# Attention beside a dense layer: a group's 64 scores in ten phases of six and seven instead of eleven phases

## The chip, the cores and the metric

The kernel runs on one core of a Trainium2 chip. The metric is the device time of one execution in microseconds (us). The program is one launch; it starts and ends with data in the chip's main memory.

## What is computed

The reference mixes two branches over the same input `x` of 2048 tokens by 512 channels: softmax attention with 32 heads of 16 channels (A), and a token-mixing MLP (B), with a gate per token.

```
qkv = x @ wqkv                                  # 32 heads, Dh = 16
scores = einsum("bhqd,bhkd->bhqk", q, k) * Dh**-0.5
o = einsum("bhqk,bhkd->bhqd", softmax(scores), v)
a = o_in_rows @ wo                              # (1, 2048, 512)

h = layernorm(x)
u = gelu(einsum("bsd,sf->bdf", h, w1) + b1)     # over tokens: 2048 -> 1792
b = einsum("bdf,fs->bds", u, w2) + b2           # 1792 -> 2048, transposed back

g = sigmoid((x * gate_w).sum(-1))
out = g * a + (1 - g) * b
```

All inputs and the output are fp32.

## The kernel before

Products that need fp32 accuracy are made of three matmuls of numbers split into a high and a low part (`hi`, `lo`). The kernel first makes v, then q and k in split form (written to main memory), then the first MLP layer with its GELU. All the rest, from about 300 us to 1290 us, is one stage in which the attention runs beside the second MLP layer and most of the output projection. The change lies in this stage alone.

*Groups.* There are `NG` = 32 groups: 16 pairs of heads times two halves of the queries. A group has 64 scores. A score (line 804) is one matmul of 64 rows: 128 keys by 512 queries of one head `i`. Head 0 sits on rows 0 to 63 of the array and head 1 on rows 64 to 127 (`i * HALF`), so a score uses half of the rows.

*Dense matmuls.* The second MLP layer and the output projection (tile `dn`, line 844) are issued as steps. Each step runs twice, once on either half of the rows, both adding to one PSUM bank. The list `dense` says which steps go with which *two*, a two being two consecutive phases; the first phase of a two (`second` = 0) runs the steps on rows 64 to 127 beside scores of head 0, the second phase the other way round. `put` fills the list, with a list of sizes per tile: `sizes_of` gives six or four for the second layer, `put_outputs` six for the projection's parts, and four at the end, where each of the last eight tiles sums the first `EARLY` = 8 of its 12 projection matmuls; `others` (line 887) does the remaining four after the attention. There are `TWOS` = 5 twos in a group, so ten phases, and behind them an eleventh phase of four scores without dense matmuls: 10 x 6 + 4 = 64.

*A phase on PE.* First its scores, each followed by a dense matmul on the other half of the rows. Where a phase has fewer dense matmuls than scores, the first scores run alone, on alternating halves. Then `apply_v` takes the exponentials of the phase before (`late`): a score's exponentials times v, two matmuls of 256 columns (line 768, 17 output rows each). Two units (scores) of the two query blocks make a pair, whose eight matmuls use four column strips of the array. The result gathers in one PSUM tile `av`, which is copied out once a group by DVE (line 731). When the phase of four has been issued, two of the three pairs that wait are taken, and the third moves on to the next phase.

*A phase on ACT.* Two scores fill one tile `s` of `ps_s`, that is two PSUM banks of 512 columns. One exponential (line 813, 128 x 1024) turns it into a tile `pt`. `ps_s` has three such tiles and `pt` six. `open_s` carries a half-filled tile from score to score.

The order of all instructions of the stage is written out by hand (`tc.manual_schedule`): each engine runs its queue in this order and waits by semaphores. POOL writes a one-element `token` after a phase's last dense matmul, and the next phase's first one waits for it, so that the two halves of the rows don't add to one bank at once.

Of the kernel before, what the change touches and what calls it, by code (L numbers as in the profile page):

```python
# [1 line left out]

# [7 lines left out]
F32 = mybir.dt.float32  # L10
# [3 lines left out]
AF = mybir.ActivationFunctionType  # L14
# [44 lines left out]
def gated_mix(ctx: ExitStack, tc: tile.TileContext, a_x, a_wqkv, a_wo, b_w1, b_b1, b_w2, b_b2, gate_w, out):  # L59
# [278 lines left out]
    with tc.tile_pool(name="ln0", bufs=3, side="right") as ln:  # L338

        def project(w, n):  # L340
            ps = bank()
            cols = slice(n * NB, (n + 1) * NB)
            hi, lo = w
            products(ps, [((hi[:, k, :], lo[:, k, :]), (xt_hi[:, k, cols], xt_lo[:, k, cols])) for k in range(ND)])
            return ps
# [178 lines left out]
    o_d = [[dram.tile([P, QW], F32, name=f"o{h}{k}") for k in range(ND)] for h in range(2)]  # L524
    r_d = [[dram.tile([P // DH, QW], F32, name=f"r{h}{k}") for k in range(ND)] for h in range(2)]
    ptp_ctx = ExitStack()
    ptp = ptp_ctx.enter_context(tc.tile_pool(name="pt", bufs=6, reuse_waits="tile"))
    psum_ctx = ExitStack()
    ps_s = psum_ctx.enter_context(tc.tile_pool(name="ps_s", bufs=3, space=PSUM, reuse_waits="tile"))
    ps_dn = psum_ctx.enter_context(tc.tile_pool(name="ps_dn", bufs=1, space=PSUM, reuse_waits="tile"))  # L530
    ps_av = psum_ctx.enter_context(tc.tile_pool(name="ps_av", bufs=1, space=PSUM, reuse_waits="tile"))
    o_parts = {}
# [97 lines left out]
    def project(t, n, m):  # L630

        box = []

        def load():
            if m == EARLY:
                row = end.tile([P, D], F32, name=f"base{t}")
            else:
                row = out_pool.tile([P, D], F32, name="row", bufs=3)
            rows[t] = load_row(row, part_d[t] if n else bp_d[t])

        def step(i):
            if i == 0:
                box.extend((ps_dn.tile([P, D], F32, name="dn"), list(o_matmuls(t // NH, t, n, m))))

            def done():
                output(t, box[0], rows[t])
                if m == 3 * ND:
                    nc.sync.dma_start(of[t * P : (t + 1) * P, :], rows[t])
                elif m != EARLY:
                    nc.sync.dma_start(part_d[t], rows[t])  # L650

            return box[0], *box[1][i], i == 0, i == m - n - 1, done if i == m - n - 1 else None

        return [(step, i) for i in range(m - n)], load

    TWOS = 5
    dense, calls = {}, {}  # L660

    def put(steps, at, sizes):
# [6 lines left out]
    def call(at, *what):  # L669
        calls.setdefault(at, []).append(what)  # L670

    def put_outputs(tiles, n, m, at, sizes=None):
        for t in tiles:
            steps, load = project(t, n, m)
            call(at - 1, load)
            at = put(steps, at, sizes or [m - n])
        return at

    def sizes_of(at, n, fours):

        sizes = [6] * n
        for i in [i for i in reversed(range(n)) if (at + i) % TWOS][:fours]:
            sizes[i] = 4
        return sizes

    EARLY = 8
    part_d = [dram.tile([P, D], F32, name=f"part{t}") for t in range(NS)]
    for k in range(ND):
        call(3 * k + 2, load_wo, k)
# [1 line left out]
    first, at = steps[:28], put(steps[28:], 0, [8, 6])  # L691
    for t in range(NS):
        if t:
            at = put(second_layer(t), at, sizes_of(at, 9, 6) if t > 9 else sizes_of(at, 8, 3))
        if t == 7:
            call(at - 8, fetch_o, 0, 0)
            call(at - 5, fetch_o, 0, 1)
            at = put_outputs(range(NH), 0, 6, at)
        if t == 10:
            call(at - 8, fetch_o, 0, 2)  # L700
            call(at - 5, fetch_o, 0, 3)
            at = put_outputs(range(NH), 6, 12, at)
    call(at - 8, fetch_o, 1, 0)
    call(at - 5, fetch_o, 1, 1)
    assert at - 5 > (NP + 8) * TWOS + 4
    call(at, open_end)
    at = put_outputs(range(NS - 3, NS), 0, 4, at)
    assert at == (NP + 12) * TWOS + 7
    call(at - 3, fetch_o, 1, 2)
    at = put_outputs(range(NH, NS - 3), 0, EARLY, at, [4, 4])  # L710
    at = put_outputs(range(NS - 3, NS), 4, EARLY, at)
    assert at == NG * TWOS
    call((NG - 1) * TWOS + 2, fetch_o, 1, 3, 3)

# [37 lines left out]

    added = [0, 0]

    def pairs_of(g, units, last):

        pairs = list(zip(*([u for u in units if u[2] == qb] for qb in range(2))))
        return [(g, pair, last and n == len(pairs) - 1) for n, pair in enumerate(pairs)]

    def apply_v(pairs):  # L760
        ot = None
# [19 lines left out]
    with tc.manual_schedule(engines=engines):  # L781
        kt, qt = {0: load_k(0)}, {0: load_q(0)}
        late, open_s, fence = [], None, None

        for n, (step, *args) in enumerate(first):
            if n and n % 12 == 0:
                split_weight(nc.vector.tensor_copy, nc.vector.tensor_tensor)
            ps, a, b, start, stop, done = step(*args)
            nc.tensor.matmul(ps, a, b, start=start, stop=stop)  # L789
            if done:  # L790
                done()

        def score(grp, i, n, done):

            nonlocal open_s
            c, qb = n // 2, (n + i) % 2
            if open_s is None:
                open_s = ps_s.tile([P, 2, NB], F32, name="s"), ptp.tile([P, 2, NB], F32, name="pt")
                m = 0
            else:  # L800
                m = 1
            s, pt = open_s
            rows = slice(i * HALF, i * HALF + ROWS)
            nc.tensor.matmul(  # L804
                s[:, m, :],
                kt[grp][rows, c * P : (c + 1) * P],
                qt[grp][rows, qb * NB : (qb + 1) * NB],
                start=True,
                stop=True,
            )  # L810
            done.append((i, c, qb, pt[:, m, :]))
            if m:
                nc.scalar.activation(pt, s, AF.Exp, scale=SCALE)  # L813
                open_s = None

        for grp in range(NG):
            at = [0, 0]
            for ph in range(2 * TWOS + 1):
                if ph == 0 and grp + 1 < NG:
                    qt[grp + 1] = load_q(grp + 1)  # L820
                if ph == 1 and grp + 1 < NG:
                    kt[grp + 1] = load_k(grp + 1)
                two, second = divmod(ph, 2)
                two += grp * TWOS
                if ph == 2 * TWOS:
                    n_s, beside = 4, []
                elif second:
                    n_s = 6
                else:
                    for what, *args in calls.get(two, ()):  # L830
                        what(*args)
                    n_s, beside = 6, [step(*args) for step, *args in dense.get(two, ())]
                units = []
                for n in range(n_s - len(beside)):
                    i = (n + second + 1) % 2
                    score(grp, i, at[i], units)
                    at[i] += 1
                half = slice(0, HALF) if second else slice(HALF, P)
                for m, (ps, a, b, first, last, done) in enumerate(beside):

                    if not 4 <= m < len(beside) - 2 or len(beside) <= n_s:
                        score(grp, second, at[second], units)
                        at[second] += 1
                    mm = nc.tensor.matmul(ps, a[half], b[half], start=first and not second, stop=last and bool(second))  # L844
                    if m == 0 and fence is not None:
                        tc.add_manual_dep(mm.ins, fence.ins.name, SYNC, reason=REASON)
                    if m == len(beside) - 1:
                        fence = nc.gpsimd.memset(token, 0.0)  # L848
                        tc.add_manual_dep(fence.ins, mm.ins.name, SYNC, reason=REASON)
                    if done and second:  # L850
                        done()
                if grp == ph == 0:
                    shift_rows(nc.vector, k_bufs[1])
                if second:
                    while stores:
                        stores.pop()()
                    if len(ready) < 2:
                        split_weight(nc.vector.tensor_copy)
                    for n, (ready_at, step) in enumerate(slow):
                        if ready_at <= two:  # L860
                            slow.pop(n)[1]()
                            break

                n = 2 if ph == 2 * TWOS and grp < NG - 1 else len(late)
                apply_v(late[:n])
                late = late[n:] + pairs_of(grp, units, ph == 2 * TWOS)
        last_ot = apply_v(late)
    psum_ctx.close()

# [3 lines left out]
    with (  # L873
# [8 lines left out]
        def others(*tiles, m=0, n=3 * ND):  # L882

            for t in tiles:
                mms = list(enumerate(o_matmuls(1, NH + t, EARLY, 3 * ND)))
                for i, (a, b) in mms[m:n]:
                    nc.tensor.matmul(pa[t], a, b, start=i == 0 and t not in LATE, stop=i == len(mms) - 1 and t in LATE)  # L887

# [142 lines left out]
```

## Time and profile before

| | |
|---|---|
| time, median of 3 runs | 1308.93 us (1307.51 to 1309.08) |
| time of the profiled execution | 1307.55 us |
| span of the profiled execution | 1305.8 us, granted TensorE clock 0.999 |
| PE (matmul) busy | 1299.0 us, 99% |
| ACT busy | 1090.6 us, 84% |
| DVE, POOL busy | 403.9 us, 200.0 us |
| exponentials | 1024 of 128 x 1024, 962.5 us busy |
| scores, av, dense halves | 2048, 8192 and some 1600 matmuls |

The span is the time from the first to the last instruction; the time of an execution has a little more around it. Busy times of PE are of a pipelined engine: a matmul's row begins at its start and ends when its last column is through, so that rows of neighbours overlap. The distance from start to start says more than the duration.

### The profile page before, as it was taken

The page shows a single profiled execution, that of the slowest core. Times are in us where ns is not written, and L with a number is a line of the kernel's source. Part 1 is how long each engine was busy: PE and PEld are TensorE (multiplying, and loading weights), DVE is VectorE, ACT ScalarE, POOL GpSimd, SP SyncE. Part 2 cuts the span into 40 slices and gives each one's busy share as a digit, 9 for nine tenths or more (in the row PEclk, how much of TensorE's full clock was granted, in tenths as well). Part 3 has the DMA queues.
Part 4 walks back from the last instruction along what each step waited for, and adds up shares of the span by engine and source line. Part 5 has one row for each costly group of instructions (what it writes and reads, how often), then busy time and mean ns, then how long its engine had stood idle before and what let it go on. Part 6 is the DMA issues. An engine that isn't in the chain of part 4 may idle for free.

```text
span 1305.8 us, 32289 instructions
## 1 busy us (share of the span) xinstructions
PE 1299.0 (99%) x13282; PEld 764.3 (59%) x13282; DVE 403.9 (31%) x538; ACT 1090.6 (84%) x1248; POOL 200.0 (15%) x467
## 2 busy tenths in 40 slices
PE   9999999999999999999999999999999999999998
PEld 7888888886555555555555555555555555454444
DVE  5775361445121111122322111232111111233324
ACT  3443343448999999999999999999999999999994
POOL 0210244453101011011000111100010101100000
PEclk9999999999999999999999999999999999999999
DMA  4497643337443333334655443545433333365522
GB/s 129 144 308 275 229 117 97 97 88 148 75 86 66 62 75 84 69 75 90 126 113 121 82 76 72 120 115 118 79 67 63 74 62 77 75 123 115 112 64 74
DMA packets 93384, 138.41 MB, mean 106 GB/s; under 512 B 14293, under 2 KB 53355, under 8 KB 90156
## 3 DMA queue, kind: packets, MB, share of 16 engines
q1 hardware_dynamic: 92652, 135.20, 44.3%
q8 instruction: 107, 1.75, 0.6%
q10 hardware_dynamic: 576, 1.05, 0.2%
q14 instruction: 49, 0.40, 0.1%
HBM read 99.63 MB, written 36.56 MB: 104 GB/s over the span
## 4 chain that ended last, share of the span: by engine, by line
PE 99%; DVE 0%; issue 0%
PE av L768 37%; PE s L804 29%; PE acc L412 12%; PE acc L73 10%; PE dn L844 10%; PE pa L887 1%; PE acc L184 1%; PE dn L789 0%; PE acc L251 0%; PE acc L228 0%; PE pa L917 0%; DVE base L930 0%; PE pa L895 0%; PE pa L894 0%; DVE idle L223 0%; PE acc L210 0%
## 5 line engine op out<-in xcount | busy, mean ns | idle before, releaser
L813 ACT ACTIVATE pt<-s 128x1024 f32<-128x1024 f32 x1024 | 962.5, 1025 | 20.9 <-PE s L804 14.9
L804 PE MATMUL s<-qs,ks 64*128 64x512 f32 x2048 | 521.3, 420 | 0.0
L768 PE MATMUL av<-pt,v 128*17 128x256 f32 x8192 | 510.6, 381 | 0.0
L804 PEld LDWEIGHTS s<-qs,ks 64*128 64x128 f32 x2048 | 297.6, 184 | 207.6 <-ACT pt L813 182.8
L768 PEld LDWEIGHTS av<-pt,v 128*17 128x17 f32 x8192 | 205.3, 97 | 259.5 <-issue 119.2
L844 PE MATMUL dn<-u_hi,w_hi 64*128 64x512 f32 x428 | 179.6, 420 | 0.0
L844 PE MATMUL dn<-u_hi,w_lo 64*128 64x512 f32 x430 | 170.2, 396 | 0.0
L844 PE MATMUL dn<-u_lo,w_hi 64*128 64x512 f32 x430 | 170.1, 396 | 0.0
L66 POOL TENSOR_TENSOR w_lo<-w_raw,w_hi 128x512 fp32r<-128x512 f32 (+1 forms) x126 | 151.7, 1205 | 115.1 <-ACT w_hi L65 108.5
L848 POOL MEMSET token<- 1x1 f32 x320 | 29.9, 93 | 873.3 <-PE dn L844 704.1
L731 DVE COPY ot<-av 128x512 f32<-128x512 f32 x31 | 21.5, 692 | 344.9 <-PE av L768 344.9
L65 ACT CAST w_hi<-w_raw 128x512 fp32r<-128x512 f32 (+1 forms) x67 | 38.1, 569 | 79.6 <-PE acc L412 58.8
L742 DVE RECIPROCAL rt<-rt 128x512 f32<-128x512 f32 x31 | 104.0, 3353 | 1.1
L412 PE MATMUL acc<-h_hi,w_hi 128*128 128x512 f32 x224 | 87.1, 389 | 0.0
L412 PE MATMUL acc<-h_lo,w_hi 128*128 128x512 f32 x224 | 87.1, 389 | 0.0
L412 PE MATMUL acc<-h_hi,w_lo 128*128 128x512 f32 x224 | 87.1, 389 | 0.0
L65 DVE CAST w_hi<-w_raw 128x512 fp32r<-128x512 f32 (+1 forms) x61 | 23.5, 387 | 190.2 <-PE s L804 82.0
L844 PEld LDWEIGHTS dn<-u_lo,w_hi 64*128 64x128 f32 x430 | 79.5, 185 | 2.5 <-POOL token L848 0.2
L844 PEld LDWEIGHTS dn<-u_hi,w_lo 64*128 64x128 f32 x430 | 79.4, 185 | 2.6
L844 PEld LDWEIGHTS dn<-u_hi,w_hi 64*128 64x128 f32 x428 | 78.8, 184 | 2.2
L73 PE MATMUL acc<-xt_hi,wc_hi 128*128 128x512 f32 x128 | 49.8, 389 | 0.0
L73 PE MATMUL acc<-xt_lo,wc_hi 128*128 128x512 f32 x128 | 49.8, 389 | 0.0
(142 smaller groups left out, 1001.5 us busy)
## 6 DMA issues: line engine op xcount, KB each, us to landing
w_raw<-in_B_w_dram SPq DMA_DIRECT2D x96, 256.0 KB
ks<-kp SPq DMA_DIRECT2D x192, 128.0 KB
qs<-qp SPq DMA_DIRECT2D x256, 64.0 KB
qp<-pc SPq DMA_DIRECT2D x16, 768.0 KB
x<-in_A_x_dram SPq DMA_DIRECT2D x32, 256.0 KB
kp<-pc SPq DMA_DIRECT2D x16, 512.0 KB
w_raw<-in_B_w_dram SPq DMA_DIRECT2D x32, 128.0 KB
bp<-row SPq DMA_DIRECT2D x16, 256.0 KB
```

The source lines that it names most:

```text
L65: copy(hi, src)
L66: return sub(lo, src, hi.bitcast(F32), ALU.subtract)
L73: nc.tensor.matmul(ps, a, b, start=start and n == 0, stop=stop and n == last)
L184: nc.tensor.transpose(turns[t][:, k, :], xs[t][:, k * P : (k + 1) * P], ident)
L412: nc.tensor.matmul(p, a, b, start=first and k == 0, stop=last and k == 2)
L731: nc.vector.tensor_copy(ot, av)
L742: nc.vector.reciprocal(rt, rt)
L768: nc.tensor.matmul(av[32 * j : 32 * j + VC, i * QC : (i + 1) * QC], v[:, c, g % NP * 2 + i, :], pt[:, h * QC : (h + 1) * QC], start=added[ ...
L804: nc.tensor.matmul(s[:, m, :], kt[grp][rows, c * P : (c + 1) * P], qt[grp][rows, qb * NB : (qb + 1) * NB], start=True, stop=True,)
L813: nc.scalar.activation(pt, s, AF.Exp, scale=SCALE)
L844: mm = nc.tensor.matmul(ps, a[half], b[half], start=first and not second, stop=last and bool(second))
L848: fence = nc.gpsimd.memset(token, 0.0)
```

## The change

A group (but the last one) gets ten phases, and two of its five twos have seven scores in each phase: 4 x 7 + 6 x 6 = 64. `SEVENS` says which twos; the default is the first and the third. Seven is odd, so in such a phase the first score has a tile of its own and an exponential of its own, of 512 columns, into one half of a tile `px`; the second phase of the two fills the other half, and the two units make a pair that is applied in the phase behind the two. The lone score's tile is used again by the sixth and seventh score of the same phase, once each half is free. The three tiles of scores are now named one by one and handed round in a deque (`banks`), and `pt` has five buffers instead of six, with `px` beside them. `apply_v` takes all that waits. The sizes of the dense steps change with the phases: seven or five in twos of seven scores, four or six in the others. Four of the last eight tiles sum nine projection matmuls early instead of eight.

```diff
-    ptp = ptp_ctx.enter_context(tc.tile_pool(name="pt", bufs=6, reuse_waits="tile"))
+    ptp = ptp_ctx.enter_context(tc.tile_pool(name="pt", bufs=5, reuse_waits="tile"))
...
-    ps_s = psum_ctx.enter_context(tc.tile_pool(name="ps_s", bufs=3, space=PSUM, reuse_waits="tile"))
+    ps_s = psum_ctx.enter_context(tc.tile_pool(name="ps_s", bufs=1, space=PSUM, reuse_waits="tile"))
...
     TWOS = 5
+    SEVENS = {0: (2, 4), 8: (2, 4), 23: (2, 4), 14: (0, 4)} | dict.fromkeys((1, 5, 9, 15, 24, 25), (1, 3))
+
+    def seven(two):
+        grp, at = divmod(two, TWOS)
+        return grp < NG - 1 and at in SEVENS.get(grp, (0, 2))
...
-    def sizes_of(at, n, fours):
-
-        sizes = [6] * n
-        for i in [i for i in reversed(range(n)) if (at + i) % TWOS][:fours]:
-            sizes[i] = 4
+    def sizes_of(at, n, total):
+
+        sizes = [7 if seven(at + i) else 4 for i in range(n)]
+        for i in reversed(range(n)):
+            if sum(sizes) > total and sizes[i] == 7:
+                sizes[i] = 5
+        for i in range(n):
+            if sum(sizes) < total and sizes[i] == 4:
+                sizes[i] = 6
         return sizes
...
-    at = put_outputs(range(NS - 3, NS), 0, 4, at)
+    whole, split_tiles = [NH + t for t in (1, 3, 5, 0, 2)], [NH + t for t in (4, 7, 6)]
+    for t in split_tiles:
+        early[t] = 9 if seven(at) else 8
+        at = put_output(t, 0, early[t] - 4, at, [early[t] - 4])
...
-    at = put_outputs(range(NH, NS - 3), 0, EARLY, at, [4, 4])
-    at = put_outputs(range(NS - 3, NS), 4, EARLY, at)
+    for t in whole:
+        sizes = [5 if seven(at + i) else 4 for i in range(2)]
+        early[t] = sum(sizes)
+        at = put_output(t, 0, early[t], at, sizes)
+    for t in split_tiles:
+        at = put_output(t, early[t] - 4, early[t], at, [4])
...
+        banks = deque(range(3))
+        lone = []
...
+        def scores(grp, n_s, second):
+            nonlocal px
+            groups = [[0], [1, 2], [3, 4], [5, 6]] if n_s == 7 else [[n, n + 1] for n in range(0, n_s, 2)]
...
+            for ns in groups:
+                if len(ns) == 1:
+                    if not second:
+                        px = ptp.tile([P, 2, NB], F32, name="px", bufs=1)
+                    x = banks.popleft()
+                    alone = ps_s.tile([P, 2, NB], F32, name=f"s{x}"), x
+                    s, pt, at_s, at_pt = alone[0], px, [0], [second]
+                elif ns[-1] == 6:
+                    (s, x), pt, at_s, at_pt = alone, ptp.tile([P, 2, NB], F32, name="pt"), [1, 0], [1, 0]
+                else:
+                    x = banks.popleft()
...
+                if len(ns) == 1:
+                    nc.scalar.activation(pt[:, second, :], s[:, 0, :], AF.Exp, scale=SCALE)
+                    lone.extend(units)
+                else:
+                    nc.scalar.activation(pt, s, AF.Exp, scale=SCALE)
+                    banks.append(x)
+                    pairs.append(pair_up(grp, *units))
+            if n_s == 7 and second:
+                pairs.insert(0, pair_up(grp, lone.pop(), lone.pop()))
+            yield pairs
...
-            for ph in range(2 * TWOS + 1):
+            last_ph = 2 * TWOS - (grp < NG - 1)
+            for ph in range(last_ph + 1):
...
-                n = 2 if ph == 2 * TWOS and grp < NG - 1 else len(late)
-                apply_v(late[:n])
-                late = late[n:] + pairs_of(grp, units, ph == 2 * TWOS)
+                apply_v(late)
+                late = pairs
+                late[-1][2] = ph == last_ph
...
-                mms = list(enumerate(o_matmuls(1, NH + t, EARLY, 3 * ND)))
+                mms = list(enumerate(o_matmuls(1, NH + t, early[NH + t], 3 * ND)))
```

More of the change, by code (lines that the diff above doesn't have):

```diff
@@ L1 @@
+from collections import deque
 from contextlib import ExitStack
@@ L634, in load @@
         def load():
-            if m == EARLY:
+            if m == early.get(t):
                 row = end.tile([P, D], F32, name=f"base{t}")
@@ L648, in done @@
                     nc.sync.dma_start(of[t * P : (t + 1) * P, :], rows[t])
-                elif m != EARLY:
+                elif m != early.get(t):
                     nc.sync.dma_start(part_d[t], rows[t])
@@ L670, in call, with put_output @@
         calls.setdefault(at, []).append(what)
[L672 to L677, printed above, removed]
-    def sizes_of(at, n, fours):
-        sizes = [6] * n
-        for i in [i for i in reversed(range(n)) if (at + i) % TWOS][:fours]:
-            sizes[i] = 4
+    def put_output(t, n, m, at, sizes):
+        steps, load = project(t, n, m)
+        call(at - 1, load)
+        return put(steps, at, sizes)
+    def sizes_of(at, n, total):
[6 more added lines that the diff above has]
+                sizes[i] = 6
+        assert sum(sizes) == total, (at, sizes)
         return sizes
-    EARLY = 8
+    early = {}
     part_d = [dram.tile([P, D], F32, name=f"part{t}") for t in range(NS)]
@@ L693, in gated_mix @@
         if t:
-            at = put(second_layer(t), at, sizes_of(at, 9, 6) if t > 9 else sizes_of(at, 8, 3))
+            n = 9 if t > 9 else 8
+            at = put(second_layer(t), at, sizes_of(at, n, 3 * NF))
         if t == 7:
@@ L697, in gated_mix @@
             call(at - 5, fetch_o, 0, 1)
-            at = put_outputs(range(NH), 0, 6, at)
+            for i in range(NH):
+                at = put_output(i, 0, 6, at, [6])
         if t == 10:
@@ L701, in gated_mix @@
             call(at - 5, fetch_o, 0, 3)
-            at = put_outputs(range(NH), 6, 12, at)
+            for i in range(NH):
+                at = put_output(i, 6, 12, at, [6])
     call(at - 8, fetch_o, 1, 0)
@@ L753, in gated_mix, with pair_up @@
     added = [0, 0]
-    def pairs_of(g, units, last):
-        pairs = list(zip(*([u for u in units if u[2] == qb] for qb in range(2))))
-        return [(g, pair, last and n == len(pairs) - 1) for n, pair in enumerate(pairs)]
+    def pair_up(g, a, b):
+        assert {a[2], b[2]} == {0, 1}
+        return [g, sorted((a, b), key=lambda u: u[2]), False]
     def apply_v(pairs):
@@ L791, in gated_mix @@
                 done()
[L793 to L814, printed above, removed]
+        def scores(grp, n_s, second):
+            nonlocal px
+            groups = [[0], [1, 2], [3, 4], [5, 6]] if n_s == 7 else [[n, n + 1] for n in range(0, n_s, 2)]
+            alone = None
+            pairs = []
+            for ns in groups:
[9 more added lines that the diff above has]
+                    x = banks.popleft()
+                    s, pt, at_s, at_pt = (
+                        ps_s.tile([P, 2, NB], F32, name=f"s{x}"),
+                        ptp.tile([P, 2, NB], F32, name="pt"),
+                        [0, 1],
+                        [0, 1],
+                    )
+                units = []
+                for m, mp in zip(at_s, at_pt):
+                    i, n = yield
+                    c, qb = n // 2, (n + i) % 2
+                    rows = slice(i * HALF, i * HALF + ROWS)
+                    nc.tensor.matmul(
+                        s[:, m, :],
+                        kt[grp][rows, c * P : (c + 1) * P],
+                        qt[grp][rows, qb * NB : (qb + 1) * NB],
+                        start=True,
+                        stop=True,
+                    )
+                    units.append((i, c, qb, pt[:, mp, :]))
+                if len(ns) == 1:
[8 more added lines that the diff above has]
+            yield pairs
@@ L816, in gated_mix @@
+        px = None
         for grp in range(NG):
             at = [0, 0]
-            for ph in range(2 * TWOS + 1):
+            last_ph = 2 * TWOS - (grp < NG - 1)
+            for ph in range(last_ph + 1):
                 if ph == 0 and grp + 1 < NG:
@@ L826, in gated_mix, with score @@
                     n_s, beside = 4, []
-                elif second:
-                    n_s = 6
-                else:
+                elif not second:
                     for what, *args in calls.get(two, ()):
                         what(*args)
-                    n_s, beside = 6, [step(*args) for step, *args in dense.get(two, ())]
-                units = []
+                    n_s, beside = 6 + seven(two), [step(*args) for step, *args in dense.get(two, ())]
+                taker = scores(grp, n_s, second)
+                next(taker)
+                def score(i):
+                    at[i] += 1
+                    return taker.send((i, at[i] - 1))
                 for n in range(n_s - len(beside)):
-                    i = (n + second + 1) % 2
-                    score(grp, i, at[i], units)
-                    at[i] += 1
+                    pairs = score((n + second + 1) % 2)
                 half = slice(0, HALF) if second else slice(HALF, P)
@@ L841, in gated_mix @@
                     if not 4 <= m < len(beside) - 2 or len(beside) <= n_s:
-                        score(grp, second, at[second], units)
-                        at[second] += 1
+                        pairs = score(second)
                     mm = nc.tensor.matmul(ps, a[half], b[half], start=first and not second, stop=last and bool(second))
```

## The prediction

> **What bounds the kernel now.** I read the page first, then the waits, then the timeline of PE and of ACT through a few phases.
>
> ```profile
> span 1305.8 us, 32289 instructions
> PE 1299.0 (99%) x13282; PEld 764.3 (59%) x13282; DVE 403.9 (31%) x538; ACT 1090.6 (84%) x1248; POOL 200.0 (15%) x467
> L813 ACT ACTIVATE pt<-s 128x1024 f32<-128x1024 f32 x1024 | 962.5, 1025 | 20.9 <-PE s L804 14.9
> ```
>
> The trace's row of line 813 adds the shortest, median and longest exponential (ns), and the start of the first and the last:
>
> ```profile
> L813 ACT ACTIVATE pt<-s x1024: 1011/1026/1057, 303.9 to 1286.3; 128x1024 f32<-128x1024 f32 x171
> ```
>
> PE looks like the bound, but the 1024 exponentials fill 962.5 us, and from the first to the end of the last are only about 983 (1287.3 - 303.9). ACT is idle 20.9 us in front of them. Two engines are close to their limits in the same stage, so I need to know how they hand over. The waits name both directions (total, times, longest):
>
> ```profile
> PEld s L804 <- ACT pt L813: 182.8, 533, 0.4
> ACT pt L813 <- PE s L804: 14.9, 91, 0.2
> ```
>
> Now the timeline of PE (start, duration). It shows three phases in a row: one with six scores beside four dense matmuls, the phase of four scores, and one with six scores beside six dense (their `dn` rows mostly left out; a `dn` row shares its start with the score beside it, since the two use different halves of the rows).
>
> ```profile
> 1162.45 0.50 PE L804 MATMUL s<-qs,ks 64*128 64x512 f32 x2
> 1162.78 0.39 PE L844 MATMUL dn<-u_hi,w_lo 64*128 64x512 f32 x1
> 1162.79 0.39 PE L804 MATMUL s<-qs,ks 64*128 64x512 f32 x1
> ...
> 1163.02 0.39 PE L804 MATMUL s<-qs,ks 64*128 64x512 f32 x1
> ...
> 1163.25 0.64 PE L804 MATMUL s<-qs,ks 64*128 64x512 f32 x2
> ...
> 1163.82 1.49 PE L768 MATMUL av<-pt,v 128*17 128x256 f32 x24
> 1165.24 0.73 PE L804 MATMUL s<-qs,ks 64*128 64x512 f32 x4
> 1165.90 1.06 PE L768 MATMUL av<-pt,v 128*17 128x256 f32 x16
> 1166.89 0.49 PE L804 MATMUL s<-qs,ks 64*128 64x512 f32 x1
> ...
> 1168.49 1.49 PE L768 MATMUL av<-pt,v 128*17 128x256 f32 x24
> 1169.91 0.50 PE L804 MATMUL s<-qs,ks 64*128 64x512 f32 x1
> ```
>
> A score and its neighbour on the other half take one slot of 0.23 us. The first phase has five slots and lasts 2.79 us (1162.45 to 1165.24), the last six slots and 3.02 (1166.89 to 1169.91). Their scores take 1.37 and 1.60, their av 1.42 each. The phase of four scores lasts 1.65 us (two slots, then 16 av in 0.99). So eight av, which is one pair of units, cost 1.42 - 0.99 = 0.43 us. What is left is fixed: 1.42 - 3 x 0.43 = 0.13 after av, and 1.60 - 6 x 0.23 = 0.22 after the scores, 0.35 us a phase.
>
> The same phase on ACT, a row of three exponentials from elsewhere, and the one weight load of the phase that waited for ACT in its middle:
>
> ```profile
> 1162.08 1.03 ACT L813 ACTIVATE pt<-s 128x1024 f32<-128x1024 f32 x1
> 1163.05 1.03 ACT L813 ACTIVATE pt<-s 128x1024 f32<-128x1024 f32 x1
> 1163.97 1.02 ACT L813 ACTIVATE pt<-s 128x1024 f32<-128x1024 f32 x1
> ```
>
> ```profile
> 318.81 2.86 ACT L813 ACTIVATE pt<-s 128x1024 f32<-128x1024 f32 x3 [0.17 <-PE s L804]
> ```
>
> ```profile
> 1163.16 0.18 PEld L804 LDWEIGHTS s<-qs,ks 64*128 64x128 f32 x1 [0.18 <-ACT pt L813]
> ```
>
> Back to back the exponentials are 0.917 us apart (2.86 less one duration of 1.026, halved; 0.92 between 1163.05 and 1163.97), so three need 2.75 of the 2.79. The first starts 0.60 after the phase does. The last one of the phase before ends at 1163.11, 0.66 into the phase; PE's weight load for the fifth score (number 4, counted from 0) starts 0.05 later and its matmul at 1163.25, 0.14 after that end. There are three score banks (pairs of PSUM banks), so a phase's third bank is free only when the third exponential of the phase before is done. In a five-slot phase number 4 is due at 0.80 anyway: the handover just fits, with nothing to spare.
>
> To check the phase lengths against the whole attention, two starts of six-slot phases with two more between them, and the evacuation of av, once a group:
>
> ```profile
> 321.00 0.49 PE L804 MATMUL s<-qs,ks 64*128 64x512 f32 x1
> ...
> 330.03 0.50 PE L804 MATMUL s<-qs,ks 64*128 64x512 f32 x1
> ```
>
> ```profile
> 337.85 0.69 DVE L731 COPY ot<-av 128x512 f32<-128x512 f32 x1 [12.07 <-PE av L768]
> ...
> 1259.80 0.69 DVE L731 COPY ot<-av 128x512 f32<-128x512 f32 x1 [5.35 <-PE av L768]
> ```
>
> Thirty groups take 921.95 us. By the lists they hold 76 twos of six dense, 74 of four, and 30 phases of four scores: 152 x 3.015 + 148 x f + 30 x 1.65 gives f = 2.80, as the rows have it (3.015 is the middle of 3.02 above and of 3.01, a third of 330.03 - 321.00). The stage is understood to 0.01 us a phase.
>
> **The change part by part.** Counting what `put` fills: before, 80 twos of six dense matmuls, 79 of four, one of eight, and 32 phases of four scores. After, as (scores, dense) of each of a two's phases: 31 (7,7), 25 (7,5), 6 (7,6), 80 (6,4), 17 (6,6), one (6,8), and one phase of four scores.
>
> Removed: 31 phases of four scores, 31 x 1.65 = 51.2 us, and 160 - 34 = 126 six-slot phases, 126 x 3.015 = 379.9. Added: two five-slot phases, 5.6; 124 phases of seven; and in each of 62 twos one more pair of av, which now falls to the phase behind the two (call it C), 62 x 0.43 = 26.7.
>
> The seven-score phases decide. PE alone would need seven slots, 3.015 + 0.225 = 3.24 us, for (7,7) and (7,6), and six, 3.015, for (7,5). ACT must do three pairs and one lone exponential of 512 columns. That one has no row; the nearest are other ACT operations of that width, and casts of two widths:
>
> ```profile
> 297.18 0.63 ACT L423 ACTIVATE gs<-gu 128x512 f32<-128x512 f32 x1 [0.94 <-DVE gu L421]
> 297.72 0.61 ACT L65 CAST w_hi<-w_raw 128x512 fp32r<-128x512 f32 x1
> 298.23 0.63 ACT L423 ACTIVATE gs<-gu 128x512 f32<-128x512 f32 x1
> L65 ACT CAST w_hi<-w_raw 128x512 fp32r<-128x512 f32 x51 | 31.6, 620 | 65.8 <-PE acc L412 49.2 <-POOL w_lo L66 15.6 <-issue 0.5
> L65 ACT CAST w_hi<-w_raw 128x256 fp32r<-128x256 f32 x16 | 6.5, 407 | 13.8 <-PE acc L412 9.6 <-issue 2.5 <-POOL w_lo L66 1.7
> ```
>
> They follow one another at 0.54 and 0.51 us. From the casts, 256 columns cost 0.213 us, so 512 fewer than the pair's bring 0.917 down to 0.49. Bounds 0.49 and 0.54; I take 0.51, because its row is a like instruction and lies between. A seven-phase costs ACT 3 x 0.917 + 0.51 = 3.26 us.
>
> The Trainium skill (ScalarE: Activation LUTs, "What ACT_TABLE_LOAD costs") speaks against the change here: an ACTIVATE has a fixed part of 186 ns beside 0.833 ns a column, and neighbours overlap by only 93 ns, so each exponential cut in two pays 93 ns again. By it the lone one would take 0.52 and a pair 0.946, which the trace contradicts (0.917); with 0.52 the sum below would be 1.2 us more.
>
> Now the handover. In a phase of seven the lone score takes bank one, numbers 1 and 2 bank two, 3 and 4 bank three; 5 and 6 go back to bank one. So the score that needs the last exponential of the phase before is number 3, not 4. In (7,5), where two scores run ahead of the dense ones, number 3 is due in the third slot, at 0.57; it gets its bank at 0.66 + 0.14 = 0.80.
> - (7,5), first phase: 0.23 late, 3.015 + 0.23 = 3.245. ACT starts the lone one at 0.60 and ends at 0.60 + 0.51 + 2 x 0.917 + 1.026 = 3.97, 0.725 into the second phase. There number 3 starts at 0.865, 0.295 late: 3.31. ACT ends 0.68 into C, whose number 4 is 0.02 late. Together 6.57.
> - (7,7): number 3 is due at 0.80, on time: 3.24. ACT ends 0.73 into the second phase, number 3 is 0.07 late: 3.31; C 0.02. Together 6.57 again: ACT and its banks set both. (7,6) has a spare place in one half that takes up the first wait: 6.57 too.
>
> So 62 x 6.57 = 407.3. C itself (3.22) leaves ACT 0.47 us of room, but it can't use it: its work for C starts when C's scores are there.
>
> What costs nothing: five `pt` buffers in place of six. The third exponential of C needs the buffer whose av ends at about 1.37 + 1.06 + 0.06 = 2.5, and is due at 0.60 + 2 x 0.917 = 2.43; the 0.07 vanish in C's room. The evacuation (0.69) still ends before the next av, since the scores between take 1.37. POOL's token lies under the 1.42 of av. Without these covers each would cost its own length, 31 or 160 times.
>
> Four tiles take one more of their last matmuls early. Two neighbours of the tail:
>
> ```profile
> 1297.46 0.40 PE L887 MATMUL pa<-wo_hi,o_hi 96*128 96x512 f32 x1
> 1297.70 0.40 PE L887 MATMUL pa<-wo_lo,o_hi 96*128 96x512 f32 x1
> ```
>
> The tail loses four at 0.24, -0.9. The early ones ride in (7,5) phases, whose length ACT sets. Behind a C, ACT is no longer late, and five-slot phases fall from 2.80 to 2.79: about 160 x 0.01 = -1.6.
>
> Sum: 407.3 + 26.7 + 5.6 - 379.9 - 51.2 - 0.9 - 1.6 = +6.0 us. The profiled execution took 1307.55 us (its span 1305.8 and 1.75 around it), so it would be 1313.6. The median of the runs is 1308.93, 1.4 above it: 1314.9, say 1315. With 0.49 or 0.54 for the lone exponential, 124 x 0.02 less or 124 x 0.03 more: +3.5 to +9.7; with 0.03 of error in the handover, at most two waits in 62 twos, 3.7 either way: 1309 to 1322 at the very ends, 1311 to 1319 for most of it.
>
> **The rivals.**
> *Only PE counts.* If the banks came back early enough (ACT shorter, or its lag carried into C), phases would last what PE needs: 25 x 6.03 + 37 x 6.48 = 390.5 in place of 407.3, so 6.0 - 16.8 = -10.8, 1298. For it: PE is 99% busy and 31 fixed parts of 0.35 fall away. Against it: the load at 1163.16 waits for ACT by name, and number 3 stands a slot earlier than number 4 did. The Trainium skill (TensorEngine Tiling (Array Packing), "Key Properties") has the rule on this side: a change of tiling mode drains the engine; the 0.35 a phase agrees. Chance 0.18, and half of it, 1306, at 0.04.
> *The reused bank waits too.* If number 5, which goes to the free half of the lone score's bank, waits for the lone exponential (ends 0.60 + 0.62 = 1.22, plus 0.14: 1.36) though due at 1.26, each seven-phase grows by 0.10 and the waits for number 3 shrink by about half of it: 62 x 0.10 = 6.2 more, 1321. It decides once that wait is for the whole bank pair. Against it: the two halves are different banks. Chance 0.12.
> *The change cancels.* All small terms at their low ends: 1309 to 1311. Chance 0.06.
>
> **How the numbers follow.** A measurement of this kernel tells about 0.2%, 2.6 us, from no change. The forecast holds 0.60, nearly all of it slower. Faster: 0.18 + 0.04 = 0.22. Same: 0.06 + 0.03 of the forecast's low end = 0.09. Slower: 0.57 + 0.12 = 0.69. The range leaves out the first rival: 1305 to 1322.
>
> **What would show it.** Right: weight loads of scores that wait for ACT at number 3 in (7,5) phases, about 0.2 us, then phases of 3.2 to 3.3 whether they hold five or seven dense; C at 3.2; lone exponentials about 0.51 from the next; no phase of four scores but the last. Wrong: (7,5) phases of 3.0 (the first rival), or a wait before number 5 (the second). A lone exponential at 0.45 or under, or a handover faster than 0.14, would break the sum.

## The result and the profile after

The changed kernel takes 1315.88 us (1315.13 to 1316.75, 6 runs) against 1308.78 before: ratio 1.0056, 95% interval 1.0043 to 1.0069, 7.1 us slower. The forecast was 1315. The profiled execution took 1315.13, its span is 1313.4, 7.6 more than before.

The page of the changed kernel, its first lines:

```profile
span 1313.4 us, 32286 instructions
PE 1304.5 (99%) x13286; PEld 758.5 (58%) x13286; DVE 404.5 (31%) x538; ACT 1095.7 (83%) x1310; POOL 198.3 (15%) x467
```

Against the page of before, ACT has 62 instructions more and is busy 5.1 us longer; PE has 31 phases fewer and is still busy 5.5 us longer. Busy shares don't say which of the two leads. The waits of weight loads for ACT do (total, times, longest):

```profile
PEld s L846 <- ACT pt L858: 153.0, 438, 0.4
```

Before it was 182.8 in 533 waits. What matters is where they stand. The timeline of a (7,5) two, some of PE's scores and the weight loads that waited, then ACT's exponentials one by one:

```profile
1054.08 0.73 PE L846 MATMUL s<-qs,ks 64*128 64x512 f32 x3
...
1054.80 0.18 PEld L846 LDWEIGHTS s<-qs,ks 64*128 64x128 f32 x1 [0.42 <-ACT pt L858]
1054.80 0.50 PE L846 MATMUL s<-qs,ks 64*128 64x512 f32 x1
...
1055.14 0.39 PE L846 MATMUL s<-qs,ks 64*128 64x512 f32 x1
1055.29 0.18 PEld L846 LDWEIGHTS s<-qs,ks 64*128 64x128 f32 x1 [0.19 <-ACT px L855]
1055.37 0.41 PE L846 MATMUL s<-qs,ks 64*128 64x512 f32 x1
...
1055.63 0.39 PE L846 MATMUL s<-qs,ks 64*128 64x512 f32 x1
...
1057.38 0.50 PE L846 MATMUL s<-qs,ks 64*128 64x512 f32 x2
...
1058.04 0.18 PEld L846 LDWEIGHTS s<-qs,ks 64*128 64x128 f32 x1 [0.37 <-ACT pt L858]
...
1058.61 0.45 PE L846 MATMUL s<-qs,ks 64*128 64x512 f32 x1
...
1058.89 0.39 PE L846 MATMUL s<-qs,ks 64*128 64x512 f32 x1
...
1060.64 0.50 PE L846 MATMUL s<-qs,ks 64*128 64x512 f32 x2
```

```profile
1053.71 1.03 ACT L858 ACTIVATE pt<-s 128x1024 f32<-128x1024 f32 x1
1054.62 0.62 ACT L855 ACTIVATE px<-s 128x512 f32<-128x512 f32 x1
1055.11 1.04 ACT L858 ACTIVATE pt<-s 128x1024 f32<-128x1024 f32 x1
```

Number 3 has its weight load at 1054.80, 0.72 into the phase, right behind the exponential that ends at 1054.74. It was due at 0.57, and the slot behind the wait takes 0.34 (to 1055.14) instead of 0.23, as the first slot of a phase does; call this a restart. The first phase lasts 3.30 us (1054.08 to 1057.38) and the second 3.26 (to 1060.64), where PE needs 3.015. The same two lengths stand in a (7,7) two, though there PE needs 3.24:

```profile
987.01 0.50 PE L846 MATMUL s<-qs,ks 64*128 64x512 f32 x1
...
990.31 0.50 PE L846 MATMUL s<-qs,ks 64*128 64x512 f32 x1
...
993.58 0.50 PE L846 MATMUL s<-qs,ks 64*128 64x512 f32 x2
...
996.79 0.50 PE L846 MATMUL s<-qs,ks 64*128 64x512 f32 x2
...
999.58 0.50 PE L846 MATMUL s<-qs,ks 64*128 64x512 f32 x1
```

3.30, 3.27, and 3.21 for C; the phase behind it, with six scores and four dense matmuls, takes 2.79. So a phase of seven costs the same with five dense matmuls as with seven. Over the whole trace the first phases of the 62 twos take 3.26 to 3.31 us (mean 3.30), the second ones 3.26 to 3.28 (mean 3.27). Thirty groups of the attention, from the evacuation of the first to that of the thirty-first:

```profile
337.57 0.69 DVE L753 COPY ot<-av 128x512 f32<-128x512 f32 x1 [10.94 <-PE av L790]
...
1266.46 0.69 DVE L753 COPY ot<-av 128x512 f32<-128x512 f32 x1 [3.51 <-PE av L790]
```

928.89 us for thirty groups, 6.9 more than the 921.95 before. From the first score to the start of the last av matmul it is 991.11 us, 6.5 more than the 984.58 before; the first group, which lies outside the thirty, got shorter.

### The profile page after: what moved, and what is told of

Its sections match the earlier page's. It is cut to its first block, busy times and chain, and to the rows that moved or that the text cites. A ratio compares the mean times of both kernels' runs of the same rounds, so it can differ in the third digit from the quotient of the medians.

```text
span 1313.4 us, 32286 instructions
## 1 busy us (share of the span) xinstructions
PE 1304.5 (99%) x13286; PEld 758.5 (58%) x13286; DVE 404.5 (31%) x538; ACT 1095.7 (83%) x1310; POOL 198.3 (15%) x467
## 4 chain that ended last, share of the span: by engine, by line
PE 99%; DMA 0%; DVE 0%; SPq 0%; issue 0%
PE av L790 37%; PE s L846 27%; PE dn L896 12%; PE acc L413 12%; PE acc L74 10%; PE acc L185 1%; PE dn L813 0%; PE pa L938 0%; PE acc L252 0%; DMA x<-in_A_x_dram 0%; PE pa L968 0%; DVE base L981 0%; SPq L177 0%; PE pa L945 0%; PE pa L946 0%; SPq L170 0%
## 5 line engine op out<-in xcount | busy, mean ns | idle before, releaser
L858 ACT ACTIVATE pt<-s 128x1024 f32<-128x1024 f32 x962 | 918.4, 1029 | 22.3 <-PE s L846 21.0
L846 PE MATMUL s<-qs,ks 64*128 64x512 f32 x2048 | 529.9, 425 | 0.0
L790 PE MATMUL av<-pt,v 128*17 128x256 f32 x7696 | 477.1, 381 | 0.0
L846 PEld LDWEIGHTS s<-qs,ks 64*128 64x128 f32 x2048 | 288.6, 184 | 220.5 <-ACT pt L858 153.0
L790 PEld LDWEIGHTS av<-pt,v 128*17 128x17 f32 x7696 | 200.2, 97 | 232.2 <-issue 88.5
L896 PE MATMUL dn<-u_hi,w_hi 64*128 64x512 f32 x428 | 174.4, 407 | 0.0
L896 PE MATMUL dn<-u_lo,w_hi 64*128 64x512 f32 x430 | 173.8, 404 | 0.0
L896 PE MATMUL dn<-u_hi,w_lo 64*128 64x512 f32 x430 | 173.3, 403 | 0.0
L855 ACT ACTIVATE px<-s 128x512 f32<-128x512 f32 x124 | 75.4, 608 | 0.0
```

The lines of the kernel that those rows point to most:

```text
L790: nc.tensor.matmul(av[32 * j : 32 * j + VC, i * QC : (i + 1) * QC], v[:, c, g % NP * 2 + i, :], pt[:, h * QC : (h + 1) * QC], start=added[ ...
L846: nc.tensor.matmul(s[:, m, :], kt[grp][rows, c * P : (c + 1) * P], qt[grp][rows, qb * NB : (qb + 1) * NB], start=True, stop=True,)
L855: nc.scalar.activation(pt[:, second, :], s[:, 0, :], AF.Exp, scale=SCALE)
```

## The experiments

Two theories stood after the result. H: a phase's third score bank comes back only when ACT has done the phase before, and ACT's lag is handed on; so each two of sevens is as long as ACT and the banks make it. P: the phases are as long as PE's own order makes them (restarts, the added pair of av). For single terms there were further rivals. The first four kernels ran together on one chip, where the kernel before took 1308.7 us.

**The changed kernel again** (no edit).

> The changed kernel once more, as the yardstick for the three runs beside it: +7 us against the kernel before (1.0054), and in its profile the time from the first matmul of the tail (pa) to the end of the span again about 18.8 us against 17.8 before, if the stores at the end are slower for a reason and not by chance; 17 to 18 if by chance.

1315.4 us, ratio 1.0052 (1.0038 to 1.0066). Thirty groups take 928.86 us, as in the other profile to 0.03. The time from the first `pa` matmul to the end is 1314.6 - 1295.99 = 18.6 us against 17.8 before, as long as in the other profile of this kernel. Whether that is more than chance is asked of the tail alone below.

**Half of the lone exponential.**

```diff
...
-nc.scalar.activation(pt[:, second, :], s[:, 0, :], AF.Exp, scale=SCALE)
+nc.scalar.activation(pt[:, second, :QC], s[:, 0, :QC], AF.Exp, scale=SCALE)
...
```

> The lone exponential takes 256 columns instead of 512 (the other half of the lone score is left out, and av uses the first half twice). Theory H (the third score bank comes back only when ACT has done the phase before, and ACT's lag is handed on from the first phase of seven to the second): ACT needs 0.21 us less in each phase of seven. The first phase of a (7,5) two keeps its wait for the phase before it (3.29), the second falls from 3.27 to about 3.06; (7,7) phases fall only to what PE needs, 0.03 to 0.05 each. Sum 25 x 0.21 + 37 x 0.08 = 8 us less than the changed kernel. Rival P (the phases are as long as PE's own order makes them): no change. Rival T (ACT's throughput alone sets a phase of seven): 124 x 0.21 = 26 us less.

1308.6 us, ratio 0.9999 (0.9990 to 1.0008): 6.8 less than the changed kernel beside it, where H said 8, for an ACT instruction that falls from 0.60 to 0.40 us. Its (7,5) two, the starts of the two phases and of C, with the sixth and the seventh score of the first phase:

```profile
1051.13 0.50 PE L846 MATMUL s<-qs,ks 64*128 64x512 f32 x2
...
1052.43 0.39 PE L846 MATMUL s<-qs,ks 64*128 64x512 f32 x1
...
1052.66 0.39 PE L846 MATMUL s<-qs,ks 64*128 64x512 f32 x1
...
1054.40 0.50 PE L846 MATMUL s<-qs,ks 64*128 64x512 f32 x2
...
1057.45 0.50 PE L846 MATMUL s<-qs,ks 64*128 64x512 f32 x2
```

3.27 and 3.05. The first phase keeps its wait, since that hangs on the phase before it; the second loses it. That is H to 0.02 us (it had 3.29 and 3.06); the (7,7) twos fell less than it said, on average by 0.05 and not 0.08. P (nothing) and a bound by ACT's throughput alone (26 us less) are out.

**The scores without a neighbour last**, in (7,5) phases; a score also picks its keys so that pairs still hold both query blocks.

```diff
...
-for n in range(n_s - len(beside)):
-    pairs = score((n + second + 1) % 2)
...
+behind = n_s == 7 and len(beside) == 5
+alone = [(n + second + 1) % 2 for n in range(n_s - len(beside))]
+for i in alone if not behind else ():
+    pairs = score(i)
...
+for i in alone if behind else ():
+    pairs = score(i)
```

> In (7,5) phases the two scores without a dense neighbour are issued behind the others instead of ahead of them, so that score number 3 is due one slot later, at 0.80 us. Which keys go with which phase shifts a little; the work is the same. Theory H: the wait of the first phase goes (3.29 to 3.02), but ACT's work is the same, so its lag turns up in the phase behind: the second phase 3.31 to 3.36, the phase behind the two 3.45 instead of 3.21. Sum within 1.5 us of the changed kernel. Rival S (each wait is a loss by itself): 25 x 0.27 = 7 us less than the changed kernel.

1313.4 us, ratio 1.0037 (1.0023 to 1.0051): 2.0 less than the changed kernel, a little more than H allowed (1.5) and far from the 7 of S, by which each wait is a loss by itself. The starts of a C, of the phase behind it, of a (7,5) two and of its second phase, with the wait inside C:

```profile
1115.51 0.50 PE L854 MATMUL s<-qs,ks 64*128 64x512 f32 x2
...
1116.41 0.18 PEld L854 LDWEIGHTS s<-qs,ks 64*128 64x128 f32 x1 [0.37 <-ACT pt L866]
...
1118.93 0.50 PE L854 MATMUL s<-qs,ks 64*128 64x512 f32 x2
...
1121.71 0.49 PE L854 MATMUL s<-qs,ks 64*128 64x512 f32 x1
...
1124.77 0.49 PE L854 MATMUL s<-qs,ks 64*128 64x512 f32 x1
```

The first phase falls to 3.06 (1121.71 to 1124.77), the second is 3.24 (by the same timeline, up to 1115.51), and C grows from 3.21 to 3.42 (1115.51 to 1118.93) with a wait at 1116.41 that it didn't have. The sum is 9.72 against 9.77. The first phase lost 0.24 us, and 0.21 of it came back in C. H had the lag come back in the right place, but put the second phase at 3.31 to 3.36; that phase, whose own order was changed too, took no more than before.

**The same, and C's too.**

```diff
-behind = n_s == 7 and len(beside) == 5
+behind = len(beside) > 3 and (n_s == 7 and len(beside) == 5 or ph % 2 == 0 and n_s == 6 and two > 0 and seven(two - 1))
```

> As alone_last, and the phase behind a two of sevens (C, six scores beside four dense) also issues its two scores without a neighbour last, so that its third bank is due at 1.03 instead of 0.80. Theory H: C can take up 0.23 us of ACT's lag without a wait: (7,5) twos with their C go from 9.77 to 9.55, 25 x 0.22 = 5.5 us less than the changed kernel; (7,7) twos stay. Rival S: the same as alone_last, 7 us less for both. Rival P: nothing in either.

1308.98 us, ratio 1.0002 (0.9993 to 1.0011): 6.4 less than the changed kernel (H: 5.5; the 7 of S lies near, but S had 7 for the kernel above too, which gained 2.0). C now takes ACT's lag without a wait. The starts of a second phase, its C, the phase behind it, the next two and its second phase:

```profile
1110.68 0.50 PE L854 MATMUL s<-qs,ks 64*128 64x512 f32 x1
...
1113.92 0.50 PE L854 MATMUL s<-qs,ks 64*128 64x512 f32 x1
...
1117.13 0.72 PE L854 MATMUL s<-qs,ks 64*128 64x512 f32 x3
...
1119.92 0.50 PE L854 MATMUL s<-qs,ks 64*128 64x512 f32 x1
...
1122.98 0.49 PE L854 MATMUL s<-qs,ks 64*128 64x512 f32 x1
```

3.06 for a first phase (1119.92 to 1122.98), 3.24 for a second, 3.21 for C: 9.51 (H: 9.55). An order of the same scores takes back nearly all of the loss.

The other four ran together; the kernel before took 1308.41.

**The tail alone**, in the kernel before.

```diff
-mms = list(enumerate(o_matmuls(1, NH + t, EARLY, 3 * ND)))
+mms = list(enumerate(o_matmuls(1, NH + t, EARLY + t % 2, 3 * ND)))
```

> The kernel before with four of the tail's projection matmuls left out (tiles 1, 3, 5 and 7 each do three of the four that line 887 does; their share of the result is missing). It is the tail of the changed kernel alone. Theory M (the prediction's: the tail lasts as long as its matmuls): 0.9 us less, and 16.9 us instead of 17.8 from the first matmul of the tail to the end of the span. Theory S (the eight stores of 256 KB set the end, and finishing closer together they get in each other's way): no gain or a loss, 17.8 to 18.7 from that matmul to the end.

1308.7 us, ratio 1.0003 (0.9994 to 1.0012). Stretches of 1 us near the end, first of this kernel (span 1307.4), then of the kernel before (PE busy, PEld, DVE, ACT, POOL, clock, DMA share, GB/s):

```profile
1300.40:1301.40 1.00, 0.00 (x0) 0.00 (x0) 0.00 (x0) 0.00 (x0) 0.00 (x0) 1.00 0.75 260
1301.40:1302.40 1.00, 0.00 (x0) 0.00 (x0) 0.00 (x0) 0.00 (x0) 0.00 (x0) 1.00 1.02 369
1302.40:1303.40 1.00, 0.00 (x0) 0.00 (x0) 0.00 (x0) 0.00 (x0) 0.00 (x0) 1.00 1.05 379
```

```profile
1301.80:1302.80 1.00, 0.00 (x0) 0.00 (x0) 0.00 (x0) 0.00 (x0) 0.00 (x0) 1.00 0.77 274
1302.80:1303.80 1.00, 0.00 (x0) 0.00 (x0) 0.00 (x0) 0.00 (x0) 0.00 (x0) 0.57 0.24 76
```

The last store is issued 12.08 us after the first `pa` matmul and not 13.02, but then the stores fill the DMA engines for three microseconds with no other engine at work; before, it was less than two. In the six profiles with the shorter tail the end comes 18.2 to 19.2 us after the first `pa` matmul, in the four with the longer one 17.8 to 18.7. From the issue of the last store to the end it is 6.1 to 7.1 us in the six and 4.8 to 5.7 in the four. M (the tail lasts as long as its matmuls) is out: nothing is gained. That it is a loss (means 18.8 and 18.2) is likely, but the two ranges overlap. Why the stores then take longer stays open. In this trace the issuing instructions of the last four stores take 1.2 to 2.2 us each, where they took 0.33 before; but in three of the six profiles with the shorter tail they all take under 0.4, so this is not the reason.

**Five buffers.**

```diff
-ptp = ptp_ctx.enter_context(tc.tile_pool(name="pt", bufs=6, reuse_waits="tile"))
+ptp = ptp_ctx.enter_context(tc.tile_pool(name="pt", bufs=5, reuse_waits="tile"))
```

> The kernel before with five buffers of exponentials instead of six. Prediction's term: nothing, since a phase's third exponential needs the buffer of the first pair of the phase before, whose av is done some 0.4 us earlier: within 1.3 us of the kernel before. Rival (the buffer holds up ACT): 0.05 to 0.1 us a phase, 352 phases, 18 us or more slower.

1308.79 us, ratio 1.0002 (0.9993 to 1.0011); thirty groups 922.07 us against 921.95. In the kernel before, it costs nothing that can be measured.

**Without the phases of four.**

```diff
...
-            for ph in range(2 * TWOS + 1):
+            for ph in range(2 * TWOS + (grp == NG - 1)):
...
```

> The kernel before without the phase of four scores in 31 groups (four scores of 64, their exponentials and av are left out). It is the term that the change removes. Prediction's term: 31 x 1.65 = 51.2 us less, and about 1 us on top, since ACT is no longer late behind these phases: 51 to 53 less. Rival (there ACT was the bound, two exponentials of 0.917): 31 x 1.83 = 56.9 less.

1258.36 us, ratio 0.9616 (0.9601 to 0.9631), 50.05 less; thirty groups 873.14 us, so a phase of four is worth (921.95 - 873.14) / 30 = 1.63. PE's 1.65 was right to 0.02, and the extra microsecond didn't come; ACT's 1.83 is out.

**Sevens only beside much dense work.** The kernel of the order above, with `SEVENS` cut to groups 0 to 10, 14 and 15, and eleven phases elsewhere.

```diff
-SEVENS = {0: (2, 4), 8: (2, 4), 23: (2, 4), 14: (0, 4)} | dict.fromkeys((1, 5, 9, 15, 24, 25), (1, 3))
+SEVENS = dict.fromkeys((2, 3, 4, 6, 7, 10, 14), (0, 2)) | dict.fromkeys((0, 8), (2, 4)) | dict.fromkeys((1, 5, 9, 15), (1, 3))
...
-            last_ph = 2 * TWOS - (grp < NG - 1)
+            last_ph = 2 * TWOS - (grp in SEVENS)
...
```

> Phases of seven only where much dense work lies beside them (groups 0 to 10, 14 and 15: 22 (7,7) and 4 (7,5) twos); the other groups keep eleven phases, and the last eight tiles their eight early matmuls. In (7,5) phases and in the phase behind a two the scores without a neighbour go last. By theory H's lengths (a (7,7) two 6.57, a (7,5) 6.33, 0.43 for the pair of av, against 6.03 and 5.59 for six scores and 1.65 for a phase of four): about 1.5 us less than the kernel before, so the same within what can be measured, 1306 to 1309 us. If the loss of the changed kernel came from something that every two of sevens pays, 26 of 62 twos would give 3 us more than the kernel before.

1307.02 us, ratio 0.9988 (0.9979 to 0.9997): 1.4 less than the kernel before, as the lengths said, and only just clear of no change.

## Why the prediction was right

- **Seven-score phases.** The handover of the third bank was the right place: number 3 waits in both (7,5) phases. The phases came out at 3.30, 3.26 and 3.21 for 3.245, 3.31 and 3.24; a two with its C at 9.77 for 9.79. Number 3 started only 0.06 behind the exponential (1054.74 to 1054.80), not 0.14, but the restart behind the wait, which the prediction didn't have, cost 0.11 more; so the first phase was longer than forecast, and the second, starting later, had less to wait for. In (7,7) number 3 was on time, as forecast, and the first phase still took 3.30 for 3.24; with half of the lone exponential these phases took 3.27 on average, and what the rest is stays open. The parts missed by 0.05 either way, and the sum of 6.57 for a two held because the misses cancel.
- **The added pair of av.** C is 0.42 longer than the phase behind it (3.21 and 2.79), for 0.43. In the trace this pair has eight rows, two for each of the four matmuls that the code gives it.
- **The lone exponential.** 0.49 us to the next start (1054.62 to 1055.11), 0.51 and 0.53 in the (7,7) two, for 0.51. The Trainium skill's figure (ScalarE: Activation LUTs, "What ACT_TABLE_LOAD costs": 186 ns + 0.833 ns a column, less 93 ns overlap, an estimate of 0.52) was as good here, while for the pairs the trace's 0.917 stands against its 0.946.
- **The attention in sum.** +6.9 us (6.0 and the 0.9 of the tail taken off again); from the first score to the last av it was 6.5 in one profile of the changed kernel and 6.7 in the other. That the thirty groups give 6.9 exactly is chance, since the forecast is for all of them.
- **The tail.** This step failed: -0.9 from four matmuls at 0.24. Up to the last store it was right. The chain of work that ended last, before and after, shows PE, then DVE, which makes the last rows for the stores (`issue` is time in which the profile shows no wait):

```profile
1297.19 3.00 PE pa L887 x12
1300.19 0.02 issue
1300.21 0.75 DVE base L930
```

```profile
1303.60 0.92 PE pa L938 x3
1304.51 0.02 issue
1304.54 2.11 DVE base L981 x3
```

The last row is done 12.98 us after the first `pa` matmul (1287.98) before, and 12.00 after it (1294.65) in the changed kernel. But the prediction took the time from there to the end as fixed, and it grew by more than was saved: 0.9 us more in both profiles (18.7 for 17.8), and no measurable change when tried alone.
- **The number.** That 1315 lies so near to 1315.88 is in part luck. The sum said 1313.6 for the profiled execution, which took 1315.13: the tail was off by 1.8, the attention by some 0.3 the other way. The 1.4 added from there to the median turned out to be 0.75.
- **What costs nothing.** Five buffers: shown by a run of the kernel before; in the changed kernel no wait of ACT for av shows in the trace. The token: PE's weight loads wait for it 0.2 us in all. The evacuation was not tried by itself.
- **The rival "only PE counts"** was refuted by the half exponential. **"The reused bank waits too"**: the wait exists, once in each phase of seven (124),

```profile
PEld s L846 <- ACT px L855: 24.3, 124, 0.2
```

but most of it is idle time of the weight loads alone. The load at 1055.29 waited, and its matmul starts at 1055.37, 0.23 behind the one before it, when it would have started anyway: the lone exponential ends 1.16 into the phase (1054.62 + 0.62), not 1.22, and number 5 was due at 1.29, not 1.26. Only the slot behind it is longer, 0.26 (to 1055.63) and in the second phase 0.28 (1058.61 to 1058.89); with half of the lone exponential it was 0.23 in the first phase (1052.43 to 1052.66). So the rival's wait costs some 0.03 to 0.05 a phase, not 0.10 and not nothing; these are part of the 3.30 and 3.27.

## What to carry to other kernels

Where two engines are within a few per cent of each other, count not only their work but the slot in which each buffer is asked for again: the change moved the reuse of the third bank one score ahead, and putting that right by order alone (in C too) gave back 6.4 of the 6.7 us. A wait that is taken away from one phase comes back in the next unless something there has both slack and a later need; here the phase behind had slack, and it became usable only when its own order was changed. Before counting a shorter tail as a gain, look at what runs after the last compute instruction.

## What was not expected of the hardware

Finishing the last rows 0.95 us earlier did not bring the stores home earlier: from the last store's issue to the end it took 4.8 us before and 6.6 us (twice) after; the reason is not known. And the attention itself repeats to 0.03 us between two executions of one kernel (928.89 and 928.86), while the first evacuation came at 337.57 and 338.95, so that the difference between these two was made before the first evacuation, most of it before the first score (303.23 and 304.37).
